# Moving the queued TensorE jobs of an attention step behind the masked scores' transposes

## The chip, the cores and the metric

The kernel runs on one core of a Trainium2 chip. The time is the device time of one execution in microseconds (us); the median of three runs is compared. A profile is one further execution, recorded by the hardware profiler. The core has TensorE (PE in the rows; its weight loads are PEld), VectorE (DVE), ScalarE (ACT), GpSimd (POOL) and SyncE, whose queue (SP) issues most of the DMAs. Each engine works through its own instructions in the order in which the program was written and waits where an instruction needs what another engine has not delivered.

## What is computed

Attention over 8 batches, 8 heads, 576 positions and 64 columns, in which each query keeps its 32 largest scores, and then a mixture of 8 experts with one expert per token. All numbers are float32.

```python
scores = scale * np.matmul(q, k.transpose(0, 1, 3, 2))          # 8 x 8 x 576 x 576
kth = np.partition(scores, -32, axis=-1)[..., -32:-31]
scores = np.where(scores >= kth, scores, -1000000000.0)
scores = scores - np.max(scores, axis=-1, keepdims=True)
attn = np.exp(scores)
attn = attn / (np.sum(attn, axis=-1, keepdims=True) + 1e-09)
x = (attn @ v), heads side by side                               # 4608 tokens x 512
expert_idx = np.argmax(x @ w_gate, axis=1)                       # 8 experts
out[mask] = gate_w[mask, None] * (np.maximum(x[mask] @ w1[e], 0.0) @ w2[e])   # per expert e
```

## The kernel before

**Attention runs in 144 steps.** A step handles two tiles of 128 queries by 576 keys; 9 steps are two pairs of heads, 18 steps are one batch. Every tile passes through a pipeline that is spread over several steps. In the loop's step t (from line 970 on) the program writes, in this order:

- `exps(t-4)`: ACT takes the exponential of nine transposed 128 x 128 blocks out of the PSUM tile `tt` (named `three` in the code, one buffer) into `et` (L452).
- `softmax(t-2, .., 0)`: ACT compares tile 0 with its threshold `nb` and writes `sg` (L423); POOL adds `sg` to the scores `sb`, which masks them (L424).
- `flush(pq)`: PE's part of the queued jobs, see below.
- `scores(t+3)`: PE multiplies queries by keys into `ps` (L354), ACT copies the result to `sb` (L356).
- `softmax(t-2, .., 1)`: the same as above for tile 1. `negate(t-1)` on POOL writes the negative row maxima `nr` (L430).
- `av(t-5)`: PE multiplies `et` by the values `rv` into `px` (L461, L476).
- `scores_left(t+3)`: PE computes the 64 leftover keys (L367 or L373), ACT copies them (L375), and SP stores the scores to DRAM.
- `transp(t-3)`: PE first writes the negative maxima into `tt` (four products, L444), then adds the nine transposed blocks of the masked scores (L447). It needs `tt` free, so `exps(t-4)` must have read it, and it needs POOL's two additions for step t-3.
- `flush(aq)`: ACT's part of the queued jobs.
- `topk(t)`: DVE finds the 32 largest of each row (L993, L997); DVE's part of the queued jobs is strewn into its second half. POOL turns the result into the threshold `nb` at the start of the next step (L973).

So DVE works on step t while ACT, POOL and PE mask and transpose the steps t-2 and t-3, and the scores are made three steps ahead.

**The jobs.** Everything that isn't in this pipeline is a generator that a planner (`advance`, called at the end of each step) moves forward piece by piece, if the piece's estimated costs fit the step's limits: turning queries and keys for the next heads (`j_prep`: PE transposes `rq`, `rk`, `lqk` into a PSUM bank `pt` or `px`, ACT copies to `qk`), sums of exponentials (`j_sums`), turning the outputs back to rows and scaling them (`j_rows`: PE multiplies `xt` by `turner`, DVE scales into `xm`, `lp`), finding and redoing rows with equal scores (`j_find`, `j_redo`, `j_patch`), and routing tokens to experts (`j_route`). A piece isn't issued at once: its PE instructions go into the list `pq`, those of ACT into `aq`, of DVE into `dq`, and the lists are emptied ("flushed") at fixed places of the next step. The job instructions are all recorded under L252, the line of a helper, and are told apart by their tiles.

After the attention steps the experts run: gathers of token rows (`gx`, `kt`), splitting of the weights in two parts, and three products for each (L1116, L1131). The steps after t = 143 and all later phases flush every list right after `advance`.

## Time and profile before

| | us |
|---|---|
| median of 3 runs (1317.35 to 1322.46) | 1319.63 |
| the profiled execution | 1320.05 |
| its span, first to last instruction | 1318.3 |
| 18 steps (one batch), from step 85's first exponential at 457.96 to step 103's at 555.20 | 97.24 |
| attention steps, about | 32 to 785 |

A row of the profile's timeline has start, duration, engine, line, operation, output tile <- input tiles, shapes and count; merged rows carry the count. A figure in square brackets is the time that the engine stood idle before the row, and who ended it. A PE row's duration overlaps the next row's, since matmuls are pipelined; what a group of matmuls costs PE is therefore read from start to start.

In the text, step numbers are those of the loop variable t. They were assigned by counting the rows of L993 (21 for each step) and of L452 and L356 (one for each step).

### The profile page before, as it was taken

The page shows a single profiled execution, that of the slowest core. Times are in us where ns is not written, and L with a number is a line of the kernel's source. Part 1 is how long each engine was busy: PE and PEld are TensorE (multiplying, and loading weights), DVE is VectorE, ACT ScalarE, POOL GpSimd, SP SyncE. Part 2 cuts the span into 40 slices and gives each one's busy share as a digit, 9 for nine tenths or more (in the row PEclk, how much of TensorE's full clock was granted, in tenths as well). Part 3 has the DMA queues.
Part 4 walks back from the last instruction along what each step waited for, and adds up shares of the span by engine and source line. Part 5 has one row for each costly group of instructions (what it writes and reads, how often), then busy time and mean ns, then how long its engine had stood idle before and what let it go on. Part 6 is the DMA issues. An engine that isn't in the chain of part 4 may idle for free.

```text
span 1318.3 us, 32644 instructions
## 1 busy us (share of the span) xinstructions
PE 1263.6 (96%) x9688; PEld 1007.0 (76%) x9688; DVE 1036.5 (79%) x6838; ACT 824.3 (63%) x1691; POOL 905.1 (69%) x1272
## 2 busy tenths in 40 slices
PE   5999999999999999999999979998899999999997
PEld 2677777777677677677676767887899999988986
DVE  6999999999999999999998975745673333345664
ACT  3998898898798798898897853433233323233442
POOL 3777887887887888888888877664654334155654
PEclk7999999999999999999999989999999999999999
DMA  6656564565655555655654525635554334256774
GB/s 173 211 158 179 171 208 141 169 186 154 173 173 165 166 170 163 172 167 168 173 167 141 158 83 146 206 93 163 159 183 145 112 105 123 80 157 186 222 218 123
DMA packets 271243, 211.25 MB, mean 160 GB/s; under 512 B 136216, under 2 KB 214216, under 8 KB 271056
## 3 DMA queue, kind: packets, MB, share of 16 engines
q1 hardware_dynamic: 260320, 185.92, 48.5%
q0 software_dynamic: 9504, 22.86, 5.4%
q8 instruction: 78, 1.28, 0.4%
q14 instruction: 109, 0.89, 0.2%
q10 hardware_dynamic: 1232, 0.30, 0.1%
HBM read 102.49 MB, written 107.90 MB: 160 GB/s over the span
## 4 chain that ended last, share of the span: by engine, by line
PE 80%; ACT 5%; issue 4%; POOL 4%; DVE 4%; DMA 2%; SPq 1%; another core or an unknown queue 0%; POOLq 0%; ACTq 0%; DVEq 0%
PE ph L1116 16%; PE y L1131 15%; PE ps L354 11%; PE px L461 10%; PE tt L447 8%; PE pt L252 8%; PE tt L444 4%; PE px L476 3%; PE px L367 2%; DVE cand L993 1%; PE mt L1096 1%; ACT sg L423 1%; ACT sb L356 1%; DMA gx<-xs,ids 1%; ACT qk L252 1%
## 5 line engine op out<-in xcount | busy, mean ns | idle before, releaser
L424 POOL TENSOR_TENSOR sb<-sb,sg 128x576 f32<-128x576 f32 x288 | 370.0, 1293 | 121.1 <-ACT sg L423 108.9
L993 DVE MAX8 cand<-sb 128x8 f32<-128x52 f32 (+2 forms) x3024 | 368.3, 207 | 1.6 <-ACT sb L356 1.1
L923 POOL TENSOR_TENSOR wl<-r,wh 128x512 fp32r<-128x512 f32 x110 | 142.3, 1295 | 222.0 <-DVE wh L922 216.5
L423 ACT ACTIVATE sg<-sb,nb 128x576 int8<-128x576 f32 x288 | 223.4, 776 | 4.7 <-POOL sb L424 4.3
L461 PEld LDWEIGHTS px<-et,rv 128*64 128x64 f32 x2688 | 132.8, 138 | 115.7 <-issue 64.1
L1117 ACT ACTIVATE hh<-ph 128x320 fp32r<-128x320 f32 (+3 forms) x136 | 58.3, 428 | 239.7 <-PE ph L1116 218.4
L997 DVE MAX8 vq<-cand 128x8 f32<-128x22 f32 (+7 forms) x1152 | 201.9, 206 | 0.1
L452 ACT ACTIVATE et<-tt 128x1152 f32<-128x1152 f32 x144 | 163.1, 1133 | 52.8 <-PE tt L447 51.9
L354 PE MATMUL ps<-qk 64*128 64x512 f32 (+1 forms) x576 | 182.2, 640 | 2.6 <-ACT sb L356 2.1
L1118 DVE SCALAR_TENSOR_TENSOR hl<-ph,hh 128x320 fp32r<-128x320 f32 (+3 forms) x136 | 65.1, 479 | 148.8 <-ACT hh L1117 124.5
L356 ACT ACTIVATE sb<-ps 128x1024 f32<-128x1024 f32 x144 | 147.3, 1023 | 50.1 <-PE ps L354 49.8
L461 PE MATMUL px<-et,rv 128*64 128x128 f32 (+1 forms) x2688 | 167.9, 268 | 9.1 <-issue 5.4
L447 PE MATMUL tt<-turner,sb 128*128 128x128 f32 x1296 | 168.2, 275 | 1.2 <-POOL sb L424 1.2
L1116 PE MATMUL ph<-xh,wh 128*128 128x320 f32 (+3 forms) x536 | 168.3, 314 | 0.0
L1116 PE MATMUL ph<-xh,wl 128*128 128x320 f32 (+3 forms) x536 | 165.1, 308 | 0.0
L1116 PE MATMUL ph<-xl,wh 128*128 128x320 f32 (+3 forms) x536 | 164.8, 307 | 0.0
L997 DVE MATCH_REPLACE8 cand<-vq,cand 128x22 f32<-128x22 f32 (+2 forms) x864 | 157.6, 189 | 0.0
L447 PEld LDWEIGHTS tt<-turner,sb 128*128 128x128 f32 x1296 | 141.0, 142 | 2.0 <-POOL sb L424 2.0
L1131 PE MATMUL y<-wh,hh 128*128 128x512 f32 x324 | 128.1, 395 | 0.5 <-ACT yo L1135 0.5
L1131 PE MATMUL y<-wh,hl 128*128 128x512 f32 x324 | 128.3, 396 | 0.0
L1131 PE MATMUL y<-wl,hh 128*128 128x512 f32 x324 | 128.2, 396 | 0.0
L1116 PEld LDWEIGHTS ph<-xh,wh 128*128 128x128 f32 x536 | 101.2, 189 | 3.6 <-issue 0.7
(245 smaller groups left out, 2385.0 us busy)
## 6 DMA issues: line engine op xcount, KB each, us to landing
r<-in_moe_w_dram SPq DMA_DIRECT2D x220, 256.0 KB
sc<-sb SPq DMA_DIRECT2D x128, 288.0 KB
sc<-sb SPq DMA_DIRECT2D x128, 256.0 KB
rv<-in_v_dram SPq DMA_DIRECT2D x32, 256.0 KB
xs<-xm SPq DMA_DIRECT2D x16, 512.0 KB
rq<-in_q_dram SPq DMA_DIRECT2D x60, 128.0 KB
rk<-in_k_dram SPq DMA_DIRECT2D x60, 128.0 KB
sc<-sb SPq DMA_DIRECT2D x32, 144.0 KB
```

The costliest lines, as they stand in the source:

```text
L354: nc.tensor.matmul(MAINS[:, n], qk[:, 0, w], qk[:, 1, 2 * LEFT:], start=True, stop=True)
L356: nc.scalar.activation(bass.AP(EX[-1].tensor, EX[-1].offset, [list(EX[-1].ap[0]), [S + LEFT, 2], [1, M]]), MAINS, AF.Copy)
L423: nc.scalar.activation(upper(SG[i]), SB[u], AF.Sign, bias=nb[:, i, 1:2], accum_out=CNT[b][:, 2 * lt + i:2 * lt + i + 1])
L424: nc.gpsimd.tensor_tensor(SB[u], SB[u], SG[i], op=OP.add)
L447: nc.tensor.matmul(tt[:, c], x[:, c * 128:(c + 1) * 128], ident, start=False, stop=c in (3, 7, 8), is_transpose=True)
L452: nc.scalar.activation(ET[t], three.rearrange("p (c q) -> p c q", c=NB9), AF.Exp, scale=0.125)
L461: yield lambda kb=kb, blk=blk: nc.tensor.matmul(px[h * 64:(h + 1) * 64], block(rv, p % 2, kb if kb < MAIN else MAIN + n, h), et[:, blk, q] ...
L923: (nc.gpsimd if i else nc.vector).tensor_tensor(lo, r, hi, op=OP.subtract)
L993: one[m][0](*one[m][1])
L997: f(*a)
L1116: nc.tensor.matmul(ph, a[:, c, :], x[:, c, s], start=(m == 0), stop=(m == len(seq) - 1))
L1131: nc.tensor.matmul(PY[u, t], a[:, s], x, start=(f == 0 and m == 0), stop=(f == FC - 1 and m == 2))
```

## The change

One line moves. PE's list of queued jobs is no longer emptied ahead of `scores`, but behind `transp`, just before ACT's list is emptied. The instructions are the same, and ACT, DVE and POOL have theirs in the same order as before.

```diff
         if grp(t - LAG):
             softmax(t - LAG, grp(t - LAG), 0)
-        flush(pq)
         scores(grp(t + LA))
         ...
         scores_left(grp(t + LA))
         if grp(t - LAG - TD):
             transp(t - LAG - TD)
+        flush(pq)
         flush(aq)
         one, two, last = topk(t, grp(t)) if grp(t) else ([], [], None)
```

In PE's order jobs still stand between transposes and the next scores. But those that were queued at the end of step t-1 stood behind the transposes of step t-1, and now stand behind those of step t. The first place is on PE, where the logits of a patch's rows (`wg` times `r_et`) follow the transposes. `r_et` is ACT's copy of what PE turned for a job one step earlier; the words in brackets name the engines whose semaphores a row waits for. Before:

```order
L447 MATMUL tt<-turner,sb 128x128 [waits Pool_49]
L447 MATMUL tt<-turner,sb 128x128 x4
L252 MATMUL pt_235<-wg,r_et 128x8 [waits Activation_49]
L252 MATMUL pt_235<-wg,r_et 128x8 x3
L354 MATMUL ps<-qk_217 128x512 x2
```

and now:

```order
L447 MATMUL tt<-turner,sb 128x128 [waits Pool_49]
L447 MATMUL tt<-turner,sb 128x128 x4
L252 MATMUL pt_235<-wg,r_et 128x8 x4
L354 MATMUL ps<-qk_217 128x512 [waits Activation_49]
L354 MATMUL ps<-qk_217 128x512
```

The products for `wg` no longer wait for ACT, since the copy was ordered ahead of an exponential for which PE has waited by then. The second place is on ACT: the queued copies of a step in which keys are turned and tokens routed (`gex` is an exponential of `j_route`, `po` a copy of its ranks, `xt` a copy of `av`'s output), and the next step's exponential behind them, as a difference:

```order
 L252 ACTIVATE gex<-sh 128x40
-L252 ACTIVATE po<-pt_236 128x40 [waits DVE_49]
-L252 ACTIVATE xt<-px 128x256
-L452 ACTIVATE et<-tt 128x1152 [waits PE_49]
+L252 ACTIVATE po<-pt_236 128x40 [waits DVE_49,PE_49]
+L252 ACTIVATE xt<-px 128x256
+L452 ACTIVATE et<-tt 128x1152
 L423 ACTIVATE sg_143,cnt<-sb,nb_221 128x576 [waits Pool_49]
 L356 ACTIVATE sb<-ps 128x2x512 [waits DMAHW3_49,DMAHW2_49,PE_49]
```

ACT's order is the same, but a queued copy that used to find its input ready now waits for PE, and the exponential, which used to wait for the transposes itself, stands behind that wait.

The third place is in step 133, on PE again: the count of the tokens of each expert (`hist` times `ones`), which DVE reads in the same step to set `skip`. Before:

```order
L447 MATMUL tt<-turner,sb 128x128 x9
L252 MATMUL pt_236<-turner,xt 128x144 x3
L252 LDWEIGHTS ones
L252 MATMUL pt_235<-hist,ones 128x8
L354 MATMUL ps<-qk_213 128x512 x2
L461 MATMUL px<-et,rv_227 64x128 x8
L476 MATMUL px<-et,rv_227 128x128
L367 MATMUL px<-qk_213 128x128
...
L447 MATMUL tt<-turner,sb 128x128 x9
L252 MATMUL pt_235<-turner,xt 128x144 x3
```

and now:

```order
L447 MATMUL tt<-turner,sb 128x128 x9
L252 MATMUL pt_236<-turner,xt 128x144 x3
L252 LDWEIGHTS ones
L252 MATMUL pt_235<-hist,ones 128x8
L354 MATMUL ps<-qk_213 128x512 x2
L461 MATMUL px<-et,rv_227 64x128 x8
L476 MATMUL px<-et,rv_227 128x128
L367 MATMUL px<-qk_213 128x128
...
L447 MATMUL tt<-turner,sb 128x128 x9
L252 MATMUL pt_235<-turner,xt 128x144 x3
L354 MATMUL ps<-qk_213 128x512 x2
L461 MATMUL px<-et,rv_227 64x64 x20
```

The rows around the count read alike. They are another step's: the transposes ahead of it are now those of step 133 itself, 13 PE rows further on in the pipeline, as the products behind the next job show (64x64 x20, which belong to step 135). DVE's instruction that reads the count stands where it stood.

## The prediction

> **What bounds the kernel now.** First the times by stage (busy time of each engine in stretches; here one batch, steps 85 to 102, in two halves), then what one engine's groups waited for in that batch, then the timelines of PE, ACT and POOL step by step, and last the chain of waits for the end of attention.

> ```profile
> core 0: us, PE busy (x) PEld busy (x) DVE busy (x) ACT busy (x) POOL busy (x), PEclk, DMA share, GB/s
> 457.93:506.60 48.67, 48.35 (x436) 35.12 (x438) 48.64 (x397) 43.93 (x92) 39.65 (x56) 1.00 0.62 184
> 506.60:555.17 48.57, 47.02 (x434) 35.34 (x429) 48.57 (x400) 38.18 (x79) 42.17 (x63) 1.00 0.53 152
> ```

> PE is busy for 95.37 of 97.24 us, DVE for 97.21. Both look full, so the question is which of them would go faster if it could. The groups of PE in this batch answer for PE: of some twenty groups only three ever waited.

> ```profile
> L461 PE MATMUL px<-et,rv 128*64 128x128 f32 (+1 forms) x336 | 21.1, 266 | 1.1 <-issue 1.1
> L252 PE MATMUL pt<-wg,r_et 128*128 128x8 f32 x8 | 1.1, 259 | 0.4 <-ACT r_et L252 0.4
> L252 PE MATMUL pt<-turner,r_sb 128*128 128x128 f32 x4 | 0.7, 286 | 0.3 <-ACT po L252 0.3
> ```

> 1.1 us is a stutter of PE's own issue, 0.4 and 0.3 us are waits for ACT in job rows. For everything else the next instruction was ready. DVE's busy time, in contrast, holds waits that look like work:

> ```profile
> 524.51 1.99 DVE L252 SCALAR_TENSOR_TENSOR r_fl<-r_li 128x1 int32<-128x1 f32 x1
> 372.39 0.25 DVE L252 TENSOR_SCALAR r_v<-eight,r_nb 128x8 f32<-128x8 f32 x1
> 373.24 0.15 DVE L252 SCALAR_TENSOR_TENSOR r_v<-r_v 128x8 f32<-128x8 f32 x1
> 763.78 1.74 DVE L252 TENSOR_SCALAR r_v<-eight,r_nb 128x8 f32<-128x8 f32 x1
> 766.08 2.56 DVE L252 SCALAR_TENSOR_TENSOR r_v<-r_v 128x8 f32<-128x8 f32 x1
> ```

> The same small operations on 8 columns take 0.25 and 0.15 us in one place and 1.74 and 2.56 in another; a single column costs 1.99. In such rows DVE is held up while POOL works, so it has some slack. I take PE as the bound of the batches.

> [...]

> **Gain: two waits of PE go.** The logits waited for ACT's copy at the end of the step before, the turned rows `r_sb` for a bank that ACT was still emptying:

> ```profile
> 355.40 1.06 PE L252 MATMUL pt<-wg,r_et 128*128 128x8 f32 x8 [0.43 <-ACT r_et L252]
> 497.86 0.66 PE L252 MATMUL pt<-turner,r_sb 128*128 128x128 f32 x4 [0.29 <-ACT po L252]
> ```

> With the jobs behind the transposes, a whole step of PE's work (4.1 us, below) lies between what ACT copies and who reads it. Each wait occurs once a batch and five times before step 130 (they start with the second batch): -0.72 x 5 = -3.6 us.

> **Cost 1: ACT's exponential stands behind the copies.** ACT's order is copies, then the next exponential `et`; the copies now wait for jobs that PE does only behind its transposes, while the exponential used to start as soon as the transposes ended. PE needs `tt` emptied by it before the next negative maxima (L444). The busiest pair of steps is 91 and 92:

> ```profile
> 486.58 0.60 PE L252 MATMUL pt<-turner,rq 128*128 128x128 f32 x4
> 487.02 1.88 PE L354 MATMUL ps<-qk 128*128 128x512 f32 x4
> 492.50 0.60 PE L252 MATMUL pt<-turner,rk 128*128 128x128 f32 x4
> 493.27 1.13 PE L354 MATMUL ps<-qk 64*128 64x512 f32 x4
> 495.90 0.65 PE L444 MATMUL tt<-identb,nr 128*128 128x512 bf16 x4
> 497.38 0.17 PE L252 MATMUL pt<-r_ok,before 128*128 128x1 bf16 x1
> ```

> ```profile
> 491.39 0.60 ACT L252 ACTIVATE qk<-pt 128x512 f32<-128x512 f32 x1
> 492.70 1.13 ACT L452 ACTIVATE et<-tt 128x1152 f32<-128x1152 f32 x1
> 496.31 0.60 ACT L252 ACTIVATE qk<-pt 128x512 f32<-128x512 f32 x1
> 497.97 1.14 ACT L452 ACTIVATE et<-tt 128x1152 f32<-128x1152 f32 x1
> 498.98 0.79 ACT L423 ACTIVATE sg<-sb,nb 128x576 int8<-128x576 f32 x1
> ```

> PE: the jobs of step 91 take 487.02 - 486.58 = 0.44, those of step 92 493.27 - 492.50 = 0.77; from scores to L444 it is 2.63 and to the next job place 4.11. ACT: copies of step 91 take 492.70 - 491.39 = 1.31, of step 92 497.97 - 496.31 = 1.66; the exponential 1.01; from exponential to the next copies 3.61. Now from the job place of step 91 on: its copies start when `rq` is turned (0.60) and end at 1.91, ACT reaches the copies of step 92 at 1.91 + 3.61 = 5.52, PE the job place of step 92 at 0.44 + 4.11 = 4.55. ACT is 0.97 late. Counted from that place, copies end at 0.97 + 1.66 = 2.63, the exponential at 3.64, and PE wants `tt` at 0.77 + 2.63 = 3.40: a wait of 0.24. In a step with copies of less than about 1.3 us there is none, by the same sum. Three other steps of the batch have as much copying. Bounds: 0, and 0.25 in each of four steps, 1.0 us. I take 0.4, since in the worked pair ACT had the largest lag: 0.4 x 5 = +2.0 us.

> **Cost 2: POOL, where it is full.** ACT's later exponential moves the comparisons `sg` and POOL's additions. In most steps the additions end well ahead of the transposes; in steps 85 to 88 POOL runs without a pause and is just in time:

> ```profile
> 461.59 1.28 POOL L424 TENSOR_TENSOR sb<-sb,sg 128x576 f32<-128x576 f32 x1 [0.38 <-ACT sg L423]
> 469.85 0.53 POOL L430 TENSOR_SCALAR nr<-vq 128x128 bf16<-128x128 f32 x1
> 466.61 0.60 PE L252 MATMUL pt<-turner,rk 128*128 128x128 f32 x4
> 467.25 1.13 PE L354 MATMUL ps<-qk 64*128 64x512 f32 x4
> 470.37 1.16 PE L447 MATMUL tt<-turner,sb 128*128 128x128 f32 x9
> ```

> The addition that step 87 needs ends at 469.85 (where the next POOL row starts), the transposes start at 470.37: 0.52 spare. Now the jobs of 467.25 - 466.61 = 0.64 stand behind these transposes, so PE arrives 0.64 earlier; and POOL's unbroken run starts later, since the exponential of step 85 waits for `wg` and a small copy behind it, 0.2 to 0.5 us behind PE. 0.64 + 0.35 - 0.52 = 0.5 us of waiting. Bounds: 0, if POOL's rows shrink by what DVE no longer holds up, and 1.4, if ACT's full lag of 0.97 and more reaches POOL. 0.5 x 5 = +2.5 us.

> **Cost 3: the count in step 133.** DVE reads it in the same step and already waits:

> ```profile
> 719.17 0.16 DVE L252 TENSOR_SCALAR skip<-pt 128x1 f32<-128x1 f32 x1 [3.58 <-PE pt L252]
> 718.36 0.75 PE pt L252 x7
> 723.31 0.74 PE pt L252 x6
> 769.39 0.20 POOL L973 TENSOR_TENSOR nb<-vq,factors 128x4 f32<-128x4 f32 x1 [0.31 <-DVE vq L997]
> 775.60 0.20 POOL L973 TENSOR_TENSOR nb<-vq,factors 128x4 f32<-128x4 f32 x1 [1.80 <-DVE vq L997]
> ```

> The count moves to the next job place, 723.31 - 718.36 = 4.95 later, and the wait grows from 3.58 to 8.5 us. Behind it DVE has the rest of its selections queued, with no idle time up to 775, and POOL's last two thresholds wait for it: here DVE sets the end of attention. But between them lie the two held-up rows at 763.78 and 766.08; DVE later by 5 us meets a POOL that waits for DVE, and gets back (1.74 - 0.25) + (2.56 - 0.15) = 3.9. Left: 5.0 - 3.9 = +1.1 us, with bounds 0 and 5.0. One more wait, 2.43 us of PE for a copy of ACT at 713.21, comes to stand behind scores that don't need it; it pays into the same place, and I leave it out of the sum.

> ```profile
> 713.21 0.66 PE L252 MATMUL pt<-turner,rk 128*128 128x128 f32 x4 [2.43 <-ACT qk L252]
> ```

> The experts' phases keep their order. **Sum:** 1320.05 (the profiled execution, 0.42 above the median of the runs) - 3.6 + 2.0 + 2.5 + 1.1 = 1322.05, so 1322 us.

> **Rivals.** *A: DVE is the bound, and its scaled rows come late.* DVE scales what PE turned in the step before:

> ```profile
> 474.50 0.55 DVE L252 TENSOR_TENSOR xm<-pt,rinv 128x384 f32<-128x384 f32 x1
> 476.30 0.90 PE L252 MATMUL pt<-turner,xt 128*128 128x144 f32 x6
> 536.69 0.41 DVE L252 TENSOR_TENSOR xm<-pt,rinv 128x256 f32<-128x256 f32 x1
> 538.20 0.60 PE L252 MATMUL pt<-turner,rq 128*128 128x128 f32 x4
> ```

> The products for 474.50 now come at 476.30 and take 0.9: DVE waits 2.7. Those for 536.69 come at 538.20 with about 1.25 of work: 2.76. If nothing absorbed that, 5.5 us for each of six batches would be +33, 1353 us. For it speaks DVE's 97.21 of 97.24. Against it: DVE that is late once stays late against PE, so the second wait swallows the first, and waits as at 524.51 shrink. Chance 0.08.

> [...]

> *B: ACT's lag is the new bound.* Both upper bounds hold (1.0 + 1.4 a batch) and the 5.0 isn't absorbed: -3.6 + 12 + 5 = +13.4, 1333 us. It decides as soon as ACT's lag reaches about 1 us in most steps with copies. For it: ACT is busy for 43.93 of 48.67 in the first half. Against it: its copies are under 1.3 us in most steps. Chance 0.22.

> *C: only the gains count.* No new waits, and PE's stutter (1.1 a batch, between two dense runs of short products of which one moves) goes as well: -3.6 - 5.5 = -9.1, 1311 us. Against it: a stutter of the issue has no wait that the change takes away. Chance 0.15.

> **From this to the numbers.** The forecast has 0.55, with a range of its own of 1316 to 1329. The range reaches from C to B, 1311 to 1334, and leaves A outside. A change of 0.5% (6.6 us) is about what can be told from none. Faster: most of C, 0.13. Slower: A, 0.17 of B and 0.06 of the forecast's upper end, 0.31. Same: 0.56.

> **What would show it.** Right: no wait in the rows of `wg` and `r_sb`; PE idle ahead of L444 in steps like 92, for ACT's exponential, by some tenths; PE waiting about half a microsecond for POOL ahead of L447 in steps like 87; `skip` waiting some 8 us and the two `r_v` rows of the last batch back near 0.2; 18 steps in 97.2 to 97.8 us. Wrong: a batch of over 99 us, with DVE idle ahead of `xm` in every batch (A) or PE idle ahead of L444 in many steps (B), or one under 96.5 (C).

## The result, and the profile after

The changed kernel takes 1331.47 us (median of 5 runs, 1329.88 to 1332.59), the kernel before 1322.46 us beside it (5 runs, 1317.35 to 1325.49). The ratio is 1.0072, with an interval of 1.0045 to 1.0099: slower by 0.7%. The profiled execution took 1330.36 us with a span of 1328.6 us, that is 10.3 us more than the span of before.

First the same batch (steps 85 to 102) in two halves, with the columns as in the prediction. It took 98.29 us in place of 97.24. PE's clock is full in both halves, and its busy time is the same (95.50 us against 95.37), so nearly all of the added microsecond is waiting.

```profile
460.37:509.50 49.13, 48.15 (x446) 34.70 (x447) 49.10 (x370) 43.89 (x94) 38.67 (x56) 1.00 0.60 178
509.50:558.66 49.16, 47.35 (x422) 35.22 (x422) 48.59 (x388) 37.42 (x80) 43.20 (x64) 1.00 0.53 153
```

What PE waits for shows in the table of waits over the whole execution (us in total, times, the longest). These are, of the kernel before, its stutter and the waits for ACT in jobs that the change was to act on:

```profile
PE px L461 <- issue: 5.4, 15, 0.5
...
PE pt L252 <- ACT qk L252: 2.4, 1, 2.4
PE pt L252 <- ACT r_et L252: 2.4, 6, 0.4
...
PE pt L252 <- ACT po L252: 1.4, 5, 0.3
```

And the rows of the changed kernel:

```profile
PE px L461 <- ACT xt L252: 9.0, 24, 1.5
...
PE pt L252 <- DVE r_qx L252: 4.3, 1, 4.3
PE tt L447 <- issue: 3.8, 7, 1.0
PE px L252 <- ACT sb L375: 3.2, 8, 0.5
...
PE tt L447 <- POOL sb L424: 1.8, 4, 0.6
...
PE tt L444 <- ACT et L452: 1.3, 1, 1.3
```

The waits for `r_et` and `po` are gone, as predicted. But the products of L461 now wait 24 times for ACT's copy `xt`, and the job `lqk` eight times for the copy of the leftover scores. Neither was in the prediction. From the third batch on, that is three waits of L461 (0.41, 0.35 and 0.21 us) and one of `lqk` (0.41 us) in each batch. The stutter has only changed its place, from L461 to L447.

One such wait in the timeline, with the end of step 87 and the start of step 88:

```profile
473.08 0.28 ACT L375 ACTIVATE sb<-px 128x128 f32<-128x128 f32 x1
...
473.15 0.60 PE L252 MATMUL pt<-turner,rk 128*128 128x128 f32 x4
...
473.59 0.27 PE L252 MATMUL px<-turner,lqk 128*128 128x128 f32 x1
...
473.79 0.60 ACT L252 ACTIVATE qk<-pt 128x512 f32<-128x512 f32 x1 [0.43 <-PE pt L252]
473.79 1.13 PE L354 MATMUL ps<-qk 64*128 64x512 f32 x4
...
474.28 0.54 ACT L252 ACTIVATE qk<-px 64x128 f32<-64x128 f32 x2
474.84 0.38 ACT L252 ACTIVATE xt<-px 128x256 f32<-128x256 f32 x1
475.12 1.12 ACT L452 ACTIVATE et<-tt 128x1152 f32<-128x1152 f32 x1
475.27 1.09 PE L461 MATMUL px<-et,rv 128*64 128x128 f32 x16 [0.35 <-ACT xt L252]
```

`xt` is the copy of the attention's output of the last two steps. It stands in the same list as the job copies, behind them, and it empties the bank `px` into which L461 writes next. ACT was free at 473.36, but the first job copy waits 0.43 us for `rk`, which PE now turns behind the transposes. Three job copies later `xt` starts at 474.84. PE is through with the scores 1.13 us after its last job and finds `px` still full.

Where the 10.3 us between the two profiled executions arose, by the first transposes (L447) of the scores of steps 0 and 126 (the loop variable is then 3 and 129) and the first product of the experts (L1116):

| stretch | before, us | after, us | difference |
|---|---|---|---|
| to the transposes of step 0 | 38.20 | 33.81 | -4.4 |
| steps 0 to 126 (seven batches) | 657.97 | 667.09 | +9.1 |
| step 126 to the experts | 108.58 | 109.85 | +1.3 |
| the experts' phase | 513.5 | 517.8 | +4.3 |

The first two batches lose 2.1 us each, the others 0.8 to 1.1 us. The gain at the start and the loss in the experts' phase come from elsewhere than the batches. At the start the jobs of the first batch wait for a load of `rq`; the scores used to stand behind them, and now they go first, so that PE is through with more when the load lands. Before and after:

```profile
25.31 1.01 PE L252 MATMUL pt<-turner,rq 128*128 128x128 f32 x2 [7.57 <-DMA rq<-in_q_dram]
```

```profile
25.24 1.04 PE L252 MATMUL pt<-turner,rq 128*128 128x128 f32 x2 [4.09 <-DMA rq<-in_q_dram]
```

At the experts the products that wait for `r_qx` waited 1.29 us before and wait 4.31 us now. Behind the longer pause the granted clock is at half. Before (two rows of the timeline, one of the windows):

```profile
802.70 0.35 PE L252 MATMUL pt<-rhs,r_qx 128*128 128x2 bf16 x8 [1.29 <-DVE r_qx L252]
...
804.75 0.38 PE L1116 MATMUL ph<-xh,rv 128*128 128x256 f32 x1 [0.74 <-ACT xh L1097]
```

```profile
804.00:808.00 4.00, 2.81 (x22) 2.60 (x22) 1.68 (x3) 1.50 (x4) 0.00 (x0) 1.00 0.81 254
```

After:

```profile
807.85 0.37 PE L252 MATMUL pt<-rhs,r_qx 128*128 128x2 bf16 x8 [4.31 <-DVE r_qx L252]
...
810.75 0.58 PE L1116 MATMUL ph<-xh,rv 128*128 128x256 f32 x1 [0.69 <-ACT xh L1097]
```

```profile
806.00:810.00 4.00, 2.15 (x17) 1.81 (x17) 2.49 (x5) 0.77 (x2) 2.69 (x2) 0.53 0.76 209
810.00:814.00 4.00, 3.17 (x14) 2.81 (x14) 1.26 (x2) 0.60 (x1) 0.00 (x0) 0.50 0.58 190
814.00:818.00 4.00, 4.00 (x20) 3.73 (x20) 2.23 (x5) 1.80 (x4) 1.30 (x1) 0.69 0.20 62
```

From 810.75 to 818 the missing clock is 3.25 x 0.50 + 4.0 x 0.31 = 2.9 us, if PE sets the pace in all of that stretch. Measured from the first product of L1116 to the first of L1131, it is less: 3.67 us before (804.75 to 808.42) and 5.77 us now (810.75 to 816.52), so 2.1 of the 4.3 us.

### The profile page after: what moved, and what is told of

It is laid out like the page before. It is cut to its first block, busy times and chain, and to the rows that moved or that the text cites. A ratio compares the mean times of both kernels' runs of the same rounds, so it can differ in the third digit from the quotient of the medians.

```text
span 1328.6 us, 32658 instructions
## 1 busy us (share of the span) xinstructions
PE 1268.2 (95%) x9688; PEld 1007.4 (76%) x9688; DVE 1039.2 (78%) x6838; ACT 820.8 (62%) x1691; POOL 906.6 (68%) x1272
## 3 DMA queue, kind: packets, MB, share of 16 engines
q8 instruction: 78, 1.28, 0.4%
## 4 chain that ended last, share of the span: by engine, by line
PE 61%; DVE 22%; ACT 6%; issue 4%; POOL 3%; DMA 2%; SPq 1%; POOLq 0%; DVEq 0%; ACTq 0%
PE ph L1116 16%; PE y L1131 16%; DVE cand L993 11%; PE px L461 6%; PE tt L447 5%; PE pt L252 5%; PE ps L354 5%; DVE cand L997 4%; DVE vq L997 4%; PE tt L444 3%; PE px L476 2%; ACT sg L423 2%; PE mt L1096 1%; PE px L367 1%; ACT qk L252 1%
## 5 line engine op out<-in xcount | busy, mean ns | idle before, releaser
L424 POOL TENSOR_TENSOR sb<-sb,sg 128x576 f32<-128x576 f32 x288 | 367.0, 1284 | 82.6 <-ACT sg L423 64.9
L423 ACT ACTIVATE sg<-sb,nb 128x576 int8<-128x576 f32 x288 | 226.3, 786 | 4.0 <-POOL sb L424 3.9
L461 PEld LDWEIGHTS px<-et,rv 128*64 128x64 f32 x2688 | 129.9, 137 | 120.6 <-ACT xt L252 42.2
L997 DVE MAX8 vq<-cand 128x8 f32<-128x22 f32 (+7 forms) x1152 | 202.3, 206 | 0.6 <-DVE vq L997 0.6
L354 PE MATMUL ps<-qk 64*128 64x512 f32 (+1 forms) x576 | 183.0, 643 | 2.6 <-ACT sb L356 2.1
L461 PE MATMUL px<-et,rv 128*64 128x128 f32 (+1 forms) x2688 | 163.3, 267 | 12.9 <-ACT xt L252 9.0
L452 ACT ACTIVATE et<-tt 128x1152 f32<-128x1152 f32 x144 | 163.4, 1134 | 17.6 <-PE tt L447 16.8
L447 PE MATMUL tt<-turner,sb 128*128 128x128 f32 x1296 | 168.3, 274 | 5.6 <-issue 3.8
L1116 PE MATMUL ph<-xh,wh 128*128 128x320 f32 (+3 forms) x536 | 169.2, 316 | 0.0
L1116 PE MATMUL ph<-xh,wl 128*128 128x320 f32 (+3 forms) x536 | 165.9, 309 | 0.3 <-DVE wl L923 0.3
L1116 PE MATMUL ph<-xl,wh 128*128 128x320 f32 (+3 forms) x536 | 165.7, 309 | 0.0
L997 DVE MATCH_REPLACE8 cand<-vq,cand 128x22 f32<-128x22 f32 (+2 forms) x864 | 157.8, 189 | 0.0
L447 PEld LDWEIGHTS tt<-turner,sb 128*128 128x128 f32 x1296 | 139.7, 141 | 8.7 <-issue 5.7
L1131 PE MATMUL y<-wh,hh 128*128 128x512 f32 x324 | 128.1, 396 | 0.7 <-ACT yo L1135 0.7
L1131 PE MATMUL y<-wl,hh 128*128 128x512 f32 x324 | 128.2, 396 | 0.0
L1131 PE MATMUL y<-wh,hl 128*128 128x512 f32 x324 | 128.2, 396 | 0.0
L1116 PEld LDWEIGHTS ph<-xh,wh 128*128 128x128 f32 x536 | 101.9, 190 | 4.0 <-issue 1.1
```

Source lines behind the costliest of these rows:

```text
L354: nc.tensor.matmul(MAINS[:, n], qk[:, 0, w], qk[:, 1, 2 * LEFT:], start=True, stop=True)
L423: nc.scalar.activation(upper(SG[i]), SB[u], AF.Sign, bias=nb[:, i, 1:2], accum_out=CNT[b][:, 2 * lt + i:2 * lt + i + 1])
L424: nc.gpsimd.tensor_tensor(SB[u], SB[u], SG[i], op=OP.add)
L447: nc.tensor.matmul(tt[:, c], x[:, c * 128:(c + 1) * 128], ident, start=False, stop=c in (3, 7, 8), is_transpose=True)
L452: nc.scalar.activation(ET[t], three.rearrange("p (c q) -> p c q", c=NB9), AF.Exp, scale=0.125)
L461: yield lambda kb=kb, blk=blk: nc.tensor.matmul(px[h * 64:(h + 1) * 64], block(rv, p % 2, kb if kb < MAIN else MAIN + n, h), et[:, blk, q] ...
```

## The experiments

Three theories stood at the start. **Theory 1:** the copy `xt` stands behind late job copies and holds up L461. **Theory 2:** DVE, which loses more to POOL than before (9.7 us in held-up rows from 458 to 555, where it lost 4.7), sets the pace of the batches. **Theory 3:** the late count of step 133 makes DVE late at the end of the attention. Each run was timed beside the kernel before; ratios are to that.

### The copies xt issued at once

```
-                act(nc.scalar.activation, XT[p][:, ...], PX, AF.Copy)
+                nc.scalar.activation(XT[p][:, ...], PX, AF.Copy)
```

(both places, L480 and L486), on the changed kernel:

> The changed kernel, with one thing taken out of the job copies' queue: ACT's copies of the attention output, xt<-px, are issued where the products (L461, L476) are, ahead of the copy of the leftover scores, and no longer behind the job copies. Theory 1 (the copy xt stands behind job copies that now end late, and PE's next products of L461 wait for it): the waits of L461 for xt, 9.0 us over the whole execution, go; a batch comes back from 98.3 to 97.3 us; the time falls from 1331.5 to about 1324 (1321 to 1327). Theory 2 (DVE, which loses 9.7 us to POOL in the batch of 458 to 555 where it lost 4.7 before, sets the pace): the waits of L461 turn into other waits, a batch stays at 98 us or more, the time at 1330 to 1333.

and on the kernel before, as a control:

> The kernel before, with the same edit of the copies xt<-px alone. Control for the run above. In the kernel before L461 waited for little (0.2 us at 150.75, 0.28 at 244.21, and no wait in the batch of 458 to 555 but the stutter), so theory 1 expects no change that can be told: 1322 (1319 to 1325). If the edit alone gains 4 us or more, the run above says little about the moved jobs.

Measured: 1512.74 us (ratio 1.143) and 1417.61 us (1.072). A third kernel, the changed one with this edit and with the jobs of step 133 early as well, was expected at about 1320 us and took 1511.08 (1.143). Both theories missed; the control shows that the edit brings a wait of its own. From its timeline:

```profile
487.79 0.37 ACT L480 ACTIVATE xt<-px 128x256 f32<-128x256 f32 x1
...
488.21 0.49 PE L367 MATMUL px<-qk 128*128 128x128 f32 x2 [0.71 <-ACT xt L480]
...
488.74 0.28 ACT L375 ACTIVATE sb<-px 128x128 f32<-128x128 f32 x1 [0.58 <-PE px L367]
```

`px` is one bank with three tenants: the output (L461), the leftover scores (L367) and the job `lqk`. A copy of one tenant holds up the products of the next (0.71 us in the row of L367). With `xt` issued ahead of the leftover scores, PE waits for ACT there every second step (60 times in the control, 52.4 us in all). Nothing follows for the theories, but the bank is now known as the place where PE and ACT meet.

### The count alone at its old place

```
+        if t == 133:
+            flush(pq)
         scores(grp(t + LA))
```

> The changed kernel, with the jobs of step 133 alone put back to their old place ahead of the scores (among them the count that skip<-pt reads). The prediction's third cost says 1.1 us less: 1330.4. Theory 3 (from step 133 on DVE sets the end of the attention, as it has no idle time behind skip until 788): the 4.25 us that DVE waits for the count go, and the experts start 4 us earlier; if PE's wait for r_qx ahead of the experts (4.31 us) shrinks by as much, the granted clock at their start stays high as well, 3 us more: 1324 to 1328. If the end is set by PE and ACT, no change: 1331.

Measured: 1329.16 us (ratio 1.0041 to 1.0069; the changed kernel has 1.0045 to 1.0099, so the times alone do not tell them apart). The profile does. From its timeline, DVE:

```profile
727.50 0.16 DVE L252 TENSOR_SCALAR skip<-pt 128x1 f32<-128x1 f32 x1 [0.24 <-PE pt L252]
...
772.21 1.74 DVE L252 TENSOR_SCALAR r_v<-eight,r_nb 128x8 f32<-128x8 f32 x1
...
774.51 2.57 DVE L252 SCALAR_TENSOR_TENSOR r_v<-r_v 128x8 f32<-128x8 f32 x1
```

The wait for the count shrinks from 4.25 us (below) to 0.24, and the two held-up rows of the last batch, which the kernel before had too, are back. From step 126 to the experts it takes 107.9 us, 2.0 less than the changed kernel, and the experts' phase takes 1326.2 - 811.55 = 514.7 us, 3.2 less. Theory 3 holds for its first part, at half of the 4 us expected: in the changed kernel the count costs about 2 us ahead of the experts. Its second part missed: the wait for `r_qx` is still 2.75 us, and the clock behind it is at 0.50 as well (808 to 816). The shorter phase goes with later pauses for gathered rows, behind which the clock was low for a shorter time in this execution (some 3.4 us at 903, where the changed kernel has 6.8 us at 902 and 3.4 us at 950). The two shorter stretches (5.2 us) lie beside 1.3 us more at the start and 1.5 us more in the batches of this execution (one batch takes 99.97 us), which is why the span is only 2.4 us shorter.

### The copies xt ahead of the job copies, behind the leftover scores

```
+    xq = []; xlate = later(xq)
...
-                act(nc.scalar.activation, XT[p]...)
+                xlate(nc.scalar.activation, XT[p]...)
...
             transp(t - LAG - TD)
-        flush(pq)
+        flush(xq); flush(pq)
         flush(aq)
```

On the changed kernel, on the kernel before (there `flush(xq)` stands ahead of `flush(aq)`), and on the changed kernel with step 133's jobs early:

> The changed kernel with the copies xt<-px in a list of their own that is issued behind the copy of the leftover scores and ahead of the job copies (the run that put them ahead of the leftover scores made L367 wait for them, since both are in one PSUM bank; here nothing of that bank is written before the next job lqk or the next L461). Theory 1 (L461 waits for xt, which stands behind late job copies): the 9.0 us of such waits go, a batch comes from 98.3 to 97.2 to 97.4 us, the experts start 6 to 8 us earlier; 1331.5 falls to about 1324 (1320 to 1327). Theory 2 (DVE's losses to POOL set the batch): the waits move to another row of PE, a batch stays at 98 us, 1330 to 1333.

> The kernel before with the same list for the copies xt<-px (ahead of the job copies, behind the copy of the leftover scores). Control: here the job copies are early, and L461 waits for xt by 0.2 us in some batches only. Theory 1: no change that can be told, 1322 (1319 to 1325). If it gains 4 us or more, the copies' order is a gain of its own and not the answer to the moved jobs.

> As the run with the xt list on the changed kernel, and with the jobs of step 133 at their old place too (alone that took the experts' start 2.0 us closer to the end of step 126's score and the experts' phase 3.2 us shorter). If the two add up: about 1320 (1316 to 1323), at the kernel before or a little under it. If DVE is ahead again once PE's batches are at 97.3, the count has less to give: 1322 to 1324.

Measured: 1326.76 us (1.0026 to 1.0052), 1324.90 us (1.0012 to 1.0039) and 1325.04 us (1.0005 to 1.0039). The list gains 4.7 us on the changed kernel and loses 2.4 on the kernel before. The waits of the first one:

```profile
PE px L252 <- ACT xt L252: 5.8, 12, 0.7
...
PE px L461 <- ACT xt L252: 0.4, 1, 0.4
```

L461 waits 0.4 us where it waited 9.0, and the seven batches take 661.4 us in place of 667.1: theory 1 is shown, for 5.7 of the 9.1 us. What is left is in part the shared bank again: `lqk` now waits for `xt` (5.8 us, where it waited 3.2 us for the leftover scores). Theory 2 falls for these batches: in the batch of 263 to 361 DVE loses 9.3 us in held-up rows (the excess over the shortest row of the same kind, counted from 0.2 us), more than the 5.6 in the changed kernel, and the batch is still shorter (97.62 us against 98.32).

In the kernel before, the list put `xt` ahead of job copies that PE waits for, and these waits grew from 2.4 and 1.4 us to:

```profile
PE pt L252 <- ACT r_et L252: 3.8, 6, 0.7
...
PE pt L252 <- ACT po L252: 2.8, 5, 0.6
```

That is 2.8 us more, the size of its loss. The early count added no gain that can be told to the xt list (1325.04 against 1326.76, with overlapping intervals); from step 126 to the experts the two take 111.0 and 110.7 us, so the 2 us of the count are there in the changed kernel and not here. The wait for `r_qx` is 4.2 and 4.3 us in them. What makes `r_qx` late stays open.

### The pause before the experts filled

```
-        pl, leave = spot("li")
+        pl, leave = spot("li"); [pe(nc.tensor.matmul, MAINS[:, i % 2], ident, turner...[:, 0:512], ...)
+                                 for i in range(7 if b == B - 1 else 0)]
```

> The changed kernel with seven matmuls of no use (identity by 512 columns, into the scores' bank that nothing reads any more, some 0.45 us each, 3.2 us) put ahead of the products that wait 4.31 us for r_qx before the experts. Theory 4 (PE's pause of 4.3 us halves the granted clock from 806 to 814, and that is why the experts' phase takes 517.9 us in place of 513.5): the clock of the experts' first 10 us stays at 1.00, their phase takes 514 to 515 us, the time falls by 3 us to about 1328.5, all else unchanged. If the phase is longer for another reason, it stays at 517 to 518, and the time at 1331 or a few tenths more.

Measured: 1329.29 us (1.0039 to 1.0075). Its timeline and windows:

```profile
807.24 6.17 PE L252 MATMUL ps<-turner 128*128 128x512 f32 x14
813.25 0.34 PE L252 MATMUL pt<-rhs,r_qx 128*128 128x2 bf16 x8
...
815.29 0.38 PE L1116 MATMUL ph<-xh,rv 128*128 128x256 f32 x1 [0.74 <-ACT xh L1097]
```

```profile
814.00:818.00 4.00, 2.81 (x22) 2.38 (x20) 1.50 (x4) 1.36 (x3) 0.00 (x0) 1.00 0.16 53
```

The matmuls took 6.17 us, not the 3.2 I had meant: each runs as two. So they end 3.1 us after `r_qx` was ready (DVE ends it at 810.1). But the clock stays at 1.00, and the experts' phase takes 1327.6 - 815.29 = 512.3 us, 5.5 less than in the changed kernel. Theory 4 is shown for the start of the phase: the pause costs PE's clock (0.50 behind it in the changed kernel from 810 to 814, 1.00 here from 814 to 818). The first product of L1131 comes 3.66 us behind the first of L1116, as in the kernel before (3.67) and 2.1 us sooner than in the changed kernel. The 5.5 us are more than that; in this execution the clock also stays at 1.00 behind two later pauses for gathered rows, where the changed kernel has 0.66 (900 to 910) and 0.85 (950 to 960). These two drops differ between the other executions as well; the last section has what the clock's records show of such drops.

### Only some jobs moved

Two kernels move a part. The first takes the kernel before and moves the jobs of the patch behind the transposes (`r_sb`, its products, the logits); the second takes the changed kernel and puts `rq`, `rk` and `lqk` back ahead of the scores (in a list `eq`, flushed there). The third is the second with step 133 early.

```
-            pe(nc.tensor.transpose, pt[...], ex[...], ident)
+            last_pe(nc.tensor.transpose, pt[...], ex[...], ident)
...
             transp(t - LAG - TD)
+        flush(lq)
         flush(aq)
```

> The kernel before, with only those jobs moved behind the transposes in whose rows PE waited, and what lies between them: the turned rows r_sb, their products with rv, and the logits with wg. All other jobs, the large copies qk among them, stay at the old place. The prediction's gain alone, with little of its cost: the waits of 0.43 (wg) and 0.29 (r_sb) go, 0.72 a batch and five batches, 3.6 us; none of these steps has a copy qk behind it that could hold up xt: 1322.5 - 3.6 = 1319 (1317 to 1321). If what a moved job costs does not depend on the copies behind it but on POOL and DVE, new waits take the gain back: 1322 to 1325.

```
-                pe(nc.tensor.transpose, pt[...], r[...], ident)
+                soon(nc.tensor.transpose, pt[...], r[...], ident)
...
+        flush(eq)
         scores(grp(t + LA))
```

> The changed kernel with the jobs rq, rk and lqk alone put back ahead of the scores, all others behind the transposes. Each of the four waits of L461 for xt in a batch had two copies qk in ACT's queue ahead of xt, and the wait of lqk for the leftover scores' bank is one of these jobs itself. Theory 1, in this sharper form (the copies qk, 1.15 us, behind late products are what costs): both groups of waits go, 9.0 and 3.2 us over the execution, the batch is at 97.2 us or under it, and 1331.5 falls to about 1321 (1318 to 1324). If other late jobs do the same, L461 keeps half of its waits: 1326 or more.

> As the run with rq, rk and lqk early, and with all jobs of step 133 early as well. If the count's cost (2 us at the experts' start, and up to 3 us of a lower clock behind it) adds to the copies' cost: 1317 (1314 to 1320), under the kernel before. If DVE's wait there is filled otherwise, as it was when the copies xt came first (1326.8 without, 1325.0 with the count early): 1320 to 1323.

Measured: 1323.13, 1339.79 (1.0103 to 1.0157) and 1340.54 us (1.0125 to 1.0166). The first kernel no longer computes the same thing: with the moved jobs in their new order part of the output comes out different, for a reason that was not found. So its time is not used. Its waits for `wg` and `r_sb` are gone, and it has the same new wait as the second, twice a batch and shorter (1.1 and 0.7 us).

All expectations missed. L461 and `lqk` wait no more for `xt` and the leftover scores in the batches, as theory 1 has it, but a wait that none of my theories had takes their place. The second kernel's waits, timeline and windows:

```profile
PE pt L252 <- DVE lp L252: 14.6, 6, 3.1
```

```profile
480.81 6.17 DVE L252 TENSOR_SCALAR r_v<-eight,r_nb 128x8 f32<-128x8 f32 x1
...
498.68 0.69 PE L252 MATMUL pt<-turner,rq 128*128 128x128 f32 x2 [2.77 <-DVE lp L252]
```

```profile
500.00:503.00 3.00, 3.00 (x4) 0.67 (x2) 3.00 (x25) 0.00 (x0) 1.43 (x2) 0.50 0.00 0
```

The job `rq` needs a bank that DVE's scaled rows (`lp`) empty. DVE is late, since one row of 8 columns was held up for 6.17 us while POOL ran without a pause. PE waits 2.77 us, then runs at half clock from about 498 to 504.5: that costs some 3 us more by estimate (half of the 6.5 us), and a batch takes 102.3 us, where the kernel before takes 97.2. Theory 2 was wrong for the changed kernel; here a late DVE does hold up the batch. With all jobs behind the transposes, `rq` comes some 4 us later and does not meet the late DVE.

### The held-up row taken away

The third of these kernels, with the four small operations that follow on `r_wk` moved from DVE to POOL, and their sums to ACT:

```
-        vec(nc.vector.tensor_scalar, v[:, 8:16], eight2, nb[:, 4:5], None, op0=OP.subtract)
...
-        vec(nc.vector.scalar_tensor_tensor, v[:, 8:16], v[:, 0:8], -BIG, v[:, 8:16], ..., accum_out=nb[:, 3:4])
+        yield need(pool=0.9)
+        pool(nc.gpsimd.tensor_scalar, v[:, 8:16], eight2, nb[:, 4:5], None, op0=OP.subtract)
...
+        yield need(act=1.4)
+        act(nc.scalar.activation, v[:, 8:16], v[:, 8:16], AF.Copy, accum_out=found[:, b:b + 1])
+        act(nc.scalar.activation, v[:, 0:8], v[:, 0:8], AF.Copy, scale=-BIG, accum_out=nb[:, 3:4])
```

> The kernel with rq, rk and lqk early and step 133 early (1340.5 us), with the four small operations that follow the maximum of r_wk on DVE (they fill r_v) done on POOL and their two sums on ACT, the same values. In that kernel PE waits 2.7 to 3.1 us for DVE's lp in every batch from the third on, and the granted clock is 0.50 for some 5 us behind it; DVE had been held for 6.17 us in a row of r_v of 8 columns while POOL ran without a pause. Theory 5 (this one held-up row makes DVE late, the late DVE holds the bank that the early rq needs, and the pause halves the clock): the waits for lp go or stay under 2.4 us, the clock stays at 1.00, a batch falls from 101.5 to 96.6 to 97.3 us, the time to 1313 to 1320, under both kernels. If the hold only moves to another small row of DVE (r_fl, po, gsm), waits and clock stay, 1335 to 1342.

Measured: 1323.85 us against 1325.99 us of the kernel before beside it, a ratio of 0.9988 with an interval of 0.9978 to 0.9999. That is 16.7 us less than the same kernel with the row on DVE (1.6% by the ratios), and a little less than the kernel before. One batch (557 to 655) of the kernel with the row on DVE, and then of this one:

```profile
557.00:655.00 98.00, 94.06 (x838) 68.26 (x833) 97.02 (x781) 78.77 (x167) 80.48 (x113) 0.98 0.56 164
```

```profile
557.00:655.00 98.00, 95.90 (x865) 69.70 (x865) 93.40 (x789) 81.96 (x175) 83.31 (x123) 1.00 0.58 167
```

And its waits:

```profile
PE tt L447 <- POOL sb L424: 7.3, 12, 0.8
PE pt L252 <- DVE r_qx L252: 5.8, 1, 5.8
PE px L461 <- ACT xt L252: 5.0, 15, 0.6
...
PE pt L252 <- DVE lp L252: 0.5, 1, 0.5
```

Theory 5 is shown: the waits for `lp` fall from 13.9 us to 0.5, the clock is full in all batches, and the seven batches take 659.2 us in place of 675.2. The edit also splits the job at another place; but `rq` still stands behind the transposes of the same step as it did, and the row `lp` that it needs comes 5.8 us earlier against these transposes, nearly as much as the row of 6.17 us was held. The batch came to 97.9 us, not the 96.6 to 97.3 that I expected. The new waits are for POOL and ACT, which carry the moved work: L447 waits for POOL (0.8 us a batch), and L461 for `xt` again (1.0 us a batch). And the wait for `r_qx` before the experts is 5.78 us. So the time missed my range (1313 to 1320) on the high side; beside this run the kernel before was itself slower than in the other sessions (1325.99 us), and the ratio puts this kernel only just under it.

## Where the prediction was right and where wrong, step by step

The forecast was 1322 us and no change that can be told, with 0.5% as the limit. The time lies inside the range (1311 to 1334), but it is slower by 0.7%, which the forecast gave a chance of 0.31. It lies where the upper end was drawn from rival B (1333 us), and that is luck: of B's parts neither the waits ahead of L444 in many steps nor those for POOL came in the batches. The two changes of most size outside the batches, -4.4 us at the start and +4.3 us in the experts' phase, were in no term and cancel each other. Of the signs named, the waits of `wg` and `r_sb` went and the `r_v` rows came back near 0.2; the others did not come, and the batch of 98.29 us lies between what was to show the forecast right (up to 97.8) and what was to show it wrong (over 99).

- **The bound was right.** PE is the bound of the batches after the change too; its busy time did not change, its waits did.
- **The gain was right:** `r_et` and `po` gave back 2.4 + 1.4 = 3.8 us, against 3.6.
- **Cost 1 failed, in its place and its size.** The lag of ACT's copies was worked out rightly, but checked against the wrong reader. I followed ACT from the copies to the exponential and put PE's deadline at L444. Between the copies and the exponential stands `xt`, and its reader L461 comes ahead of L444 in the step, right behind the scores. The term of +2.0 measures 9.0 us of waits for `xt` (7.5 of them in the seven batches), and 1.3 us ahead of L444, once in the execution. The edit of the list shows 5.7 us of it in the batches' time. The upper bound, 0.25 in each of four steps or 1.0 us a batch, is near the 0.97 us a batch that came, but at another reader; and the first two batches have 1.3 us of such waits each, where I counted five batches only.
- **One term was missing:** `lqk` writes the bank of the leftover scores and now comes close behind these: 3.2 us.
- **Cost 2 was too high.** L447 waits 1.8 us for POOL in the whole execution (1.2 us before), all of it from step 132 on and none in steps 85 to 88. The lower bound, 0, was right, and its ground shows in the rows: the addition L424 at 468.08 took 1.80 us in the kernel before, beside DVE's `r_wk` (1.11 us from 467.63), and from 460 to 481 of the changed kernel all additions take 1.27 to 1.29 us.
- **Cost 3 was right in kind.** I expected `skip` to wait 8.5 us and the two `r_v` rows to give 3.9 us back. From the timeline of the changed kernel:

```profile
728.74 0.16 DVE L252 TENSOR_SCALAR skip<-pt 128x1 f32<-128x1 f32 x1 [4.25 <-PE pt L252]
...
771.64 2.85 DVE L252 TENSOR_TENSOR r_wk<-sg,r_sb 128x576 f32<-128x576 bf16 x1
```

  DVE came later itself, so the wait grew by 0.7 us only. The rows `r_v` did shrink to 0.21 us and less, but `r_wk` ahead of them grew to 2.85 (0.84 to 1.11 in the five batches before). The count costs about 2 us to the experts' start by the run with step 133 early, against +1.1 (bounds 0 and 5.0).
- **The experts' phase does not keep its time:** it lost 4.3 us, 2.1 of them since the longer wait for `r_qx` (4.31 us, with the clock at 0.50 from 810 to 814) halved PE's clock at its start. The prediction costed it at nothing because its order does not change. The rest goes with the two later drops of the clock (0.66 over 900 to 910, 0.85 over 950 to 960), which differ between executions; it was not measured apart.
- **The start** gained 4.4 us in the profiled execution. Kernels with `rq` late reach the transposes of step 0 at 33.7 to 36.0 us and those with `rq` early at 36.7 to 38.9. I had looked only at batches from the second on.
- **Rival A did not happen** in the changed kernel: DVE has no waits ahead of `xm` of the kind in the batches (from 247 us on at most 0.5 us). PE is busy for 95.50 of 98.29 us, and with the waits added to it the batch is 1.05 us longer. **Rival C's** stutter did not go; it moved to L447 and is about as long.

The sum, mended by what was measured: 1320.05 - 3.8 + 9.0 + 3.2 + 2.0 - 4.4 + 4.3 = 1330.35, against 1330.36 in the profiled execution. That fit is luck. The list gave back only 5.7 of the 9.0 us; 1.5 of these 9.0 and 0.8 of the 3.2 us lie outside the seven batches; and waits that came and went behind step 126 (2.43 us for `qk` and 3.43 us for `lp` are gone, 2.59 us for `hist` are new) are not in the sum.

## What to carry to other kernels

When work is moved later in an in-order queue, list everything queued behind the copies that follow it, and for each the first reader on the other engine; the nearest deadline decides, not the largest operation. A PSUM bank with several tenants couples them: here the copy `xt` held up L461 (9.0 us in the changed kernel), L367 (52.4 us in the control) or `lqk` (5.8 us with the list), whichever list it was put in. And a pause of the matmul engine is to be priced twice where a slow clock follows it, as here behind waits of 2.59 us (0.50 for 3.4 us) and 4.31 us (0.50 for 10.2 us): once as the wait and once as the slow clock.

## What the runs showed of the chip

**A pause can halve the clock, and its length alone doesn't decide.** Behind a wait of 2.59 us the clock fell to 0.50. From the changed kernel's timeline and windows:

```profile
784.96 0.23 PE L252 MATMUL pt<-hist,before 128*128 128x40 bf16 x1 [2.59 <-DVE hist L252]
```

```profile
786.00:789.00 3.00, 3.00 (x21) 2.16 (x18) 1.38 (x6) 2.43 (x5) 1.68 (x3) 0.50 0.47 158
```

Other waits left it at 1.00: 2.43 us for `qk` in the kernel before (at 713.21) and 2.07 us for `r_et` in the changed kernel (at 792.82). And a pause of 1.41 us (at 948.43 of the changed kernel) was followed by half clock from 949.58 on, while one of 1.41 us in the kernel before (at 940.09) was not.

**A small row of DVE can be held up over many POOL instructions.** In the kernel with the early jobs the row of 6.17 us (480.81 to 486.98) spans a run of POOL from 480.87 to 486.89: two iotas, two thresholds `nb`, four additions L424 and a `nr`. The same row took 0.25 us at 372.39 of the kernel before. There, each of the 12 DVE rows between 45 and 790 us that took at least 0.9 us more than the shortest of their kind lies with 95% or more of its time in busy rows of POOL, and in the changed kernel each of the 14 with 97% or more. The traces show these rows side by side; what holds DVE up in them is not shown.
